# Output product of each attention block in two parts, a halved PSUM copy and an earlier first row transfer

## The chip, the cores and the metric

The kernel runs on one core of one Trainium2 chip. The metric is device time in microseconds of one execution: 1679.77 us, the median of three runs (1678.62 to 1679.84). Five engines appear in the profile: PE (matrix products; PEld is its weight load), DVE (vector engine), ACT (scalar engine), POOL (GpSimd) and SP, which only issues transfers.

## The reference

For x of 2048 rows and 512 columns, 32 heads of 16, and an inner width F of 1792:

```python
x = A_x
mod = (_silu(c) @ w_mod).reshape(c.shape[0], 6, 1, -1)
sa, ca, ga, sb, cb, gb = (mod[:, 0], ..., mod[:, 5])
h = _layernorm(x, axis=-1) * (1 + ca) + sa
x = x + ga * _A_ref(h, A_wqkv, A_wo)      # softmax attention over all rows, then @ wo
h = _layernorm(x, axis=-1) * (1 + cb) + sb
x = x + gb * _B_ref(h, B_w1, B_b1, B_w2)  # dense, bias, h * tanh(softplus(h)), dense
return x
```

## The kernel before

Every fp32 operand of a large product is split into a high and a low part, and three products (high with high, high with low, low with high) stand for one. The query rows are taken in four blocks of 512. The attention is a loop of **steps** t, written by hand: 16 steps per group of heads, 128 per block, 512 in all, with a prologue of 20. A filled step holds, for PE:

- four score products (L519), each followed by an exponential on ACT (L527);
- four products of the head group 20 steps ahead (L478), whose row maxima DVE takes (L480); they are the number that softmax subtracts;
- the product of probabilities and values of two steps before (L547), written as eight matmuls that I call *pv*; the profile shows them as one row with x8;
- up to six half products (64 of the 128 contraction rows, L132) of one **unit** of other work, each run beside a score or a maximum product in the other half of the array.

The units wait in a first-in first-out queue (L1104), each with a time from which it may start; `next_part` (L1110) hands six half products to each step, or three in the last 20 steps, where no maxima are left. `h` in the code counts half steps. A block qb has these units, which run during the steps of the block after it:

- *wo* i = 0 to 3: the attention's output product of 128 rows, 12 products, thus 24 halves or four steps. The result lies in the single bank "ms". `fin` (L832 to L850) copies it to the single buffer `yd` on ACT (L834), POOL adds it to row tile y (L835), and three half steps later the layer norm begins (`norm_y`, L702): a mean pass on ACT over y with an accumulated sum (L708), a squared pass (L712) two half steps on, small POOL operations (L709, L713, L714) and the normed tile on POOL (L715).
- *tr* i: the transposition of that normed tile by eight small PE matmuls behind pv (L856). ACT copies its result out of PSUM (L861), POOL scales and shifts it (L864, four operations) and splits it (L95, L98) into `h`.
- *up* f = 0 to 13: the first dense product; it needs all four `h` tiles. A chain on ACT, DVE and POOL forms the activation and splits it.
- *down* (group, i): the second dense product over a group of f. ACT or DVE copies to `yd` (L906), POOL adds it to y (L907). Group 4 of a block runs between the next block's *wo* and *up* units.

The last query block has no loop behind it. Its output product, layer norm and dense layers stand in the **tail** (L1004 to L1095), which PE reads in order: the output product (L1020), then *down* units of the third block that were **held** for this place (L126 products into two ring banks, DVE adds them at L903), transpositions of the four normed tiles (L1055), the scale, shift and split of these (L719, L95, L98), more held units, and then up and down products alternating. Ten *down* units are held: six of them before the transpositions.

A further transfer concerns the start: the negated maxima of a head group are transposed (L497), copied by ACT (L500, L501), added by POOL (L502), and `put` (L504 to L511) issues four SP transfers of them to `qa`, which the score products read.

## Time and profile before

| quantity | value |
|---|---|
| median of three runs | 1679.77 us (1678.62 to 1679.84) |
| the profiled execution's own time | 1677.17 us |
| its span in the trace | 1675.4 us |
| granted PE clock | 1.00 |
| PE busy, share of the span | 1649.3 us, 98% |
| DVE busy | 1425.7 us, 85% |
| ACT busy | 1336.4 us, 80% |
| POOL busy | 910.9 us, 54% |

The profile gives each engine's busy time, the chain of work that ended last, groups of instructions by line, and a timeline. In a timeline a row starts with the time in us from the span's start and the duration in us; then follow engine, line, operation, destination and sources, and the number of merged instructions. A bracket at the end gives the engine's idle time before the row and what ended it. Matmul ends are modelled and overlap their successors, so the length of a step is read from the start of one pv row to the start of the next.

### The profile page before, as it was taken

The numbers are of one execution on the slowest core, as the hardware profiler recorded it, in microseconds if no ns is written. First come the engines' busy times: TensorE is split into PE (matmuls) and PEld (weight loads), VectorE is DVE, ScalarE is ACT, GpSimd is POOL, SyncE is SP. The second block draws the span as 40 slices with busy tenths as digits, with TensorE's granted clock in tenths as the row PEclk, the third lists the DMA queues.
The fourth block names the chain that finished last, engine by engine and source line by source line (L and its number), as shares of the span: only waits on it lengthen the run. The fifth ranks groups of instructions, "written<-read, shape, count | busy, mean of one in ns | idle before, by whom it ended". The sixth has DMA issues, their size and how long they took to land.

```text
span 1675.4 us, 33101 instructions
## 1 busy us (share of the span) xinstructions
PE 1649.3 (98%) x12316; PEld 921.4 (55%) x12316; DVE 1425.7 (85%) x2327; ACT 1336.4 (80%) x2625; POOL 910.9 (54%) x938
## 2 busy tenths in 40 slices
PE   7999999999999999999999999999999999999999
PEld 5755665555435455555555555555555555554687
DVE  6888898888998988888888888888888888882577
ACT  6257778787779899888889898888889889889364
POOL 5155215465434398854535498654535597645532
PEclk9999999999999999999999999999999999999999
DMA  7677456777684443435343644334442645332362
GB/s 253 186 224 226 110 168 198 236 229 226 201 254 113 111 107 86 119 78 160 86 126 75 200 105 97 102 108 121 121 102 72 178 104 134 87 116 84 126 228 73
DMA packets 113992, 240.03 MB, mean 143 GB/s; under 512 B 24048, under 2 KB 49648, under 8 KB 107784
## 3 DMA queue, kind: packets, MB, share of 16 engines
q1 hardware_dynamic: 113832, 237.92, 50.4%
q8 instruction: 97, 1.59, 0.4%
q14 instruction: 63, 0.52, 0.1%
HBM read 179.95 MB, written 51.44 MB: 138 GB/s over the span
## 4 chain that ended last, share of the span: by engine, by line
PE 83%; POOL 5%; DMA 4%; ACT 4%; DVE 2%; SPq 1%; issue 1%; ACTq 0%; DVEq 0%; POOLq 0%
PE bk L547 27%; PE ring L478 22%; PE ring L519 21%; PE bk L132 6%; PE ring L126 2%; ACT pr L527 2%; PE ring L1088 2%; DMA ka<-kscr 1%; PE bk L126 1%; DVE mx L480 1%; DMA wr<-in_A_wqkv 1%; DMA xt<-in_A_x 1%; POOL rr L781 1%; POOL ee L779 1%; POOL hb L786 1%
## 5 line engine op out<-in xcount | busy, mean ns | idle before, releaser
L480 DVE TENSOR_REDUCE mx<-ring 128x1 f32<-128x512 f32 x2048 | 1278.8, 684 | 159.5 <-PE bk L132 96.0
L527 ACT ACTIVATE pr<-ring 128x512 f32<-128x512 f32 x2048 | 1087.8, 603 | 197.9 <-PE bk L132 159.8
L478 PE MATMUL ring<-ka,qa 64*128 64x512 f32 x2048 | 773.9, 425 | 1.5 <-ACT pr L527 0.8
L519 PE MATMUL ring<-qa,ka 64*128 64x512 f32 x2048 | 719.3, 395 | 6.6 <-ACT pr L527 4.9
L478 PEld LDWEIGHTS ring<-ka,qa 64*128 64x128 f32 x2048 | 365.9, 184 | 396.0 <-DVE mx L480 351.6
L547 PE MATMUL bk<-pr,vg 128*32 128x512 f32 x4096 | 545.1, 604 | 0.0
L519 PEld LDWEIGHTS ring<-qa,ka 64*128 64x128 f32 x2048 | 374.3, 184 | 113.8 <-ACT pr L527 37.7
L132 PE MATMUL bk<-h,w 64*128 64x512 f32 x1008 | 279.9, 409 | 0.0
L132 PE MATMUL bk<-w,a_h 64*128 64x512 f32 x576 | 194.7, 417 | 1.2 <-ACT pr L527 0.6
L132 PEld LDWEIGHTS bk<-h,w 64*128 64x128 f32 x1008 | 171.5, 184 | 2.9 <-ACT yd L906 0.9
L547 PEld LDWEIGHTS bk<-pr,vg 128*32 128x32 f32 x4096 | 80.9, 108 | 127.2 <-issue 120.0
L132 PE MATMUL bk<-w,a_l 64*128 64x512 f32 x288 | 113.9, 396 | 0.0
L749 POOL TENSOR_SCALAR ee<-hb 128x512 f32<-128x512 f32 x42 | 62.5, 1488 | 93.6 <-ACT hb L743 85.1
L132 PEld LDWEIGHTS bk<-w,a_h 64*128 64x128 f32 x576 | 95.4, 185 | 5.3 <-ACT pr L527 1.8
L779 POOL TENSOR_TENSOR ee<-ee,rr 128x512 f32<-128x512 f32 x42 | 54.0, 1285 | 75.5 <-ACT rr L770 75.3
L132 PE MATMUL bk<-w,o_hl 64*128 64x512 f32 x288 | 79.5, 408 | 0.0
L98 POOL TENSOR_TENSOR a_l<-hb,a_h 128x512 fp32r<-128x512 f32 x53 | 71.7, 1354 | 4.4
L907 POOL TENSOR_TENSOR y<-yd,y 128x512 f32<-128x512 f32 x40 | 51.5, 1287 | 28.2 <-ACT yd L906 28.0
L502 POOL TENSOR_TENSOR mt<-mt,mh 32x128 fp32r<-32x128 f32 x32 | 14.4, 450 | 87.9 <-ACT mh L501 87.9
L132 PE MATMUL bk<-h_h,wl 64*128 64x512 f32 x168 | 56.8, 418 | 0.0
L787 POOL TENSOR_TENSOR hb<-hb,rr 128x512 f32<-128x512 f32 x42 | 54.5, 1298 | 3.3
L764 POOL TENSOR_TENSOR ee<-ee,rr 128x512 f32<-128x512 f32 x42 | 54.0, 1287 | 3.5
(211 smaller groups left out, 1847.9 us busy)
## 6 DMA issues: line engine op xcount, KB each, us to landing
ka<-kscr SPq DMA_DIRECT2D x124, 384.0 KB
w<-w2scr SPq DMA_DIRECT2D x56, 512.0 KB
w<-w1scr SPq DMA_DIRECT2D x46, 512.0 KB
vg<-vscr SPq DMA_DIRECT2D x32, 552.0 KB
qa<-qscr SPq DMA_DIRECT2D x124, 100.0 KB
kscr<-qh SPq DMA_DIRECT2D x16, 512.0 KB
qscr<-qh SPq DMA_DIRECT2D x32, 256.0 KB
w1scr<-hl SPq DMA_DIRECT2D x14, 512.0 KB
```

The source lines that it names most:

```text
L98: (nc.gpsimd if eng == "p" else nc.vector).tensor_sub(lo, src, hi.bitcast(F32))
L132: i = nc.tensor.matmul(acc, l[64 * g:64 * g + 64], r[64 * g:64 * g + 64], start=start, stop=stop)
L478: nc.tensor.matmul(pm, qt[64 * s:64 * s + 64, qs * P:(qs + 1) * P], kt[64 * s:64 * s + 64, kb * TB:(kb + 1) * TB], start=True, stop=True)
L480: return nc.vector.tensor_reduce(out=mxs[n][:, s, 4 * j + qs, kb:kb + 1], in_=pm, op=ALU.max, axis=AX.X)
L519: nc.tensor.matmul(p_, kt[64 * s:64 * s + 64, kc * P:(kc + 1) * P], qt[64 * s:64 * s + 64, :], start=True, stop=True)
L527: e = nc.scalar.activation(pr, p_, AF.Exp, scale=SCALE)
L547: nc.tensor.matmul(accs[n][32 * h:32 * h + 32, :], vgs[n][:, o:o + 32], pts.pop((t, h)), start=(kc == 0), stop=(kc == 15))
L749: nc.gpsimd.tensor_scalar_min(buf("ee", 2), b["hb"], HCAP)
L764: nc.gpsimd.tensor_mul(ee, ee, rr)
L779: nc.gpsimd.tensor_mul(ee, ee, rr)
L787: nc.gpsimd.tensor_mul(hb, hb, rr)
L907: nc.gpsimd.tensor_add(y[i], yd, y[i])
```

## The change

Five edits, in three groups:

1. **The output product in two parts.** A unit `part(i)` takes the contraction tiles 0 and 1, and `wo(i)` the tiles 2 and 3. The four `part` units stand in the queue behind *down*(4,0) and ahead of the four `wo` units, and may start before the block's last heads are done. Each part has its own copy on ACT, which also accumulates a row sum (L830), and its own add on POOL (L831). The row mean comes from these sums and from the stored mean of x (POOL, L832), so the mean pass L708 of before is gone; the squared pass follows three half steps after the copy of `wo(i)`, and *tr* 1 to 3 wait for 7 half steps from it as before, *tr* 0 for 5.
   As a consequence every *up* and *down* unit of blocks 0 to 2 stands 8 steps earlier in the loop: block 0's *up* 0 at step 150 instead of 158, block 1's at 278 instead of 286, block 2's at 406 instead of 414. The number of steps ahead of the last 20 without any half product falls from 28 to 20, and *down*(2,2) and *down*(2,3) of the third block move from the tail into steps 496 to 511. The tail holds eight units, five ahead of the transpositions.
2. **The copy of a transposed tile** is halved: DVE copies the first 64 rows of the tile, ACT the rest.
3. **The first heads' rows**: for the first head group the add stands on DVE instead of POOL, and `put` one half step earlier. A row load of y moves from 20 to 11 half steps behind *down*(4,0).

```diff
-    def norm_y(y):
...
-        def mean():
-            nc.scalar.activation(xn, y, AF.Identity, accum_out=ss[:, 0:1])
-            nc.gpsimd.tensor_scalar(ss[:, 1:2], ss[:, 0:1], -1.0 / D, 0.0, op0=ALU.mult, op1=ALU.add)
...
+    def norm_y(y, ss):
+        xn = mst["p"].tile([P, D], F32, tag="hb", name="xn2", bufs=3)
+        nc.scalar.activation(xn, y, AF.Square, bias=ss[:, 1:2], accum_out=ss[:, 2:3])
...
-        def wo_unit(i, tag):
+        def wo_unit(i, tag, ks):
...
-                nc.scalar.copy(yd, acc)
+                nc.scalar.activation(yd, acc, AF.Identity, accum_out=part)
                 nc.gpsimd.tensor_add(y[i], yd, y[i])
...
+                nc.gpsimd.tensor_scalar(m, part, -1.0 / D, xmean[:, 4 * qb + i:4 * qb + i + 1] if ks[0] == 0 else ss[i][:, 0:1],
+                                        op0=ALU.mult, op1=ALU.add)
+                if ks[0] == 0:
+                    return
...
-                nc.scalar.copy(hf.rearrange("p k (g m) -> p g k m", g=2),
-                               acc[:, :, :256].rearrange("p g (k m) -> p g k m", k=DK))
+                for g, eng in enumerate((nc.vector.tensor_copy, nc.scalar.copy)):
+                    eng(hf[:, :, 64 * g:64 * g + 64], acc[:, g, :256].rearrange("p (k m) -> p k m", k=DK))
...
-                    load(h + 20, then["y"], lambda j: load_y(qb + 1, j), range(3, 4))
+                    load(h + 11, then["y"], lambda j: load_y(qb + 1, j), range(3, 4))
...
+        def part(i):
+            queue(lambda: 0 if qb else done.get("w", 4 * T) + 4, lambda tag: wo_unit(i, tag, range(2)))
+
         def wo(i):
-            queue(lambda: max(t0, done.get("w", 0 if qb else 4 * T)), lambda tag: wo_unit(i, tag))
+            queue(lambda: t0, lambda tag: wo_unit(i, tag, range(2, DK)))
...
-            mst["held"] = lambda j, acc: down_unit(2 + (j + 2) // 4, (j + 2) % 4, None, acc)
+            mst["held"] = lambda j, acc: down_unit(3 + j // 4, j % 4, None, acc)
...
+            for i in range(4):
+                b["units"]["part"](i)
...
-        nc.gpsimd.tensor_add(mt, mc, mh.bitcast(F32))
+        (nc.gpsimd if n else nc.vector).tensor_add(mt, mc, mh.bitcast(F32))
...
-        at(2 * (16 * n + 16 - PRO) + 3, put)
+        at(2 * (16 * n + 16 - PRO) + (3 if n else 2), put)
...
-        fins = held((4, 5))
+        fins = held((4,))
...
-        for js in ((6, 7), (8, 9)):
+        for js in ((5, 6), (7,)):
```

Three places show the order of instructions. First ACT, in block 1's attention loop's following stage, before the change, behind the copy of the first *wo* result (`yd`; `pr` are exponentials, `xn` and `ln_s` the norm's tiles, `y_5280` the row tile):

```order
L834 COPY yd<-bk 128x512
L527 ACTIVATE pr_0_1175<-ring 128x512
L527 ACTIVATE pr_0_1182<-ring 128x512
...
L708 ACTIVATE xn_9910,ln_s<-y_5280 128x512
L527 ACTIVATE pr_1_1183<-ring 128x512
L527 ACTIVATE pr_2_1177<-ring 128x512
L527 ACTIVATE pr_2_1184<-ring 128x512
L527 ACTIVATE pr_2_1151<-ring 128x512
L712 ACTIVATE xn_9910,ln_s<-y_5280,ln_s 128x512
```

The same place after the change, from the copy of one `wo` result to that of the next:

```order
L830 ACTIVATE yd,ln_s<-bk 128x512
L529 ACTIVATE pr_1_1177<-ring 128x512
L529 ACTIVATE pr_1_1184<-ring 128x512
...
L529 ACTIVATE pr_2_1178<-ring 128x512
L706 ACTIVATE xn_9943,ln_s<-y_5281,ln_s 128x512
L529 ACTIVATE pr_2_1185<-ring 128x512
L830 ACTIVATE yd,ln_s<-bk 128x512
```

The mean pass is gone, and the squared pass of one tile stands a single exponential ahead of the copy of the next tile's result. Next POOL in the same stage, before, from the add of the second tile (`gate_97` serves as a row tile) to that of the third:

```order
L835 TENSOR_TENSOR gate_97<-yd,gate_97 128x512
L864 TENSOR_SCALAR hf_10008<-hf_10008,modc 128x128 x4
L95 TENSOR_SCALAR h_9994<-hf_10008 128x4x128
L98 TENSOR_TENSOR h_9995<-hf_10008,h_9994 128x4x128
L709 TENSOR_SCALAR ln_s<-ln_s 128x1
L713 TENSOR_SCALAR ln_s<-ln_s 128x1
L714 TENSOR_TENSOR ln_s<-ln_s,nhalf 128x1
L715 TENSOR_SCALAR xn_10052<-gate_97,ln_s 128x512
L835 TENSOR_TENSOR gate_98<-yd,gate_98 128x512
```

And after the change, from the add of the third tile to that of the fourth:

```order
L831 TENSOR_TENSOR gate_99<-yd,gate_99 128x512
L832 TENSOR_SCALAR ln_s<-ln_s 128x1
L862 TENSOR_SCALAR hf_10055<-hf_10055,modc 128x128 x4
L96 TENSOR_SCALAR h_10045<-hf_10055 128x4x128
L99 TENSOR_TENSOR h_10046<-hf_10055,h_10045 128x4x128
L707 TENSOR_SCALAR ln_s<-ln_s 128x1
L708 TENSOR_TENSOR ln_s<-ln_s,nhalf 128x1
L709 TENSOR_SCALAR xn_10100<-gate_99,ln_s 128x512
L831 TENSOR_TENSOR y_5277<-yd,y_5277 128x512
```

POOL has the same sequence per tile as before, but the `wo` results now arrive every two steps instead of every four. Last DVE in the tail, before, behind the last normed tile (`pr`); L903 is the add of a held unit, L98 the low part of `h`:

```order
L109 TENSOR_SCALAR pr_1_1158<-pr_0_1157,ln_mv,ln_rs 128x512
L903 TENSOR_TENSOR y_5279<-ring,y_5279 128x512
L903 TENSOR_TENSOR y_5280<-ring,y_5280 128x512
...
L903 TENSOR_TENSOR y_5279<-ring,y_5279 128x512
L903 TENSOR_TENSOR y_5280<-ring,y_5280 128x512
L98 TENSOR_TENSOR h_17796<-hf_17829,h_17795 128x512
```

And after:

```order
L110 TENSOR_SCALAR pr_1_1159<-pr_0_1158,ln_mv,ln_rs 128x512
L901 TENSOR_TENSOR y_5278<-ring,y_5278 128x512
L901 TENSOR_TENSOR y_5279<-ring,y_5279 128x512
L901 TENSOR_TENSOR y_5280<-ring,y_5280 128x512
L901 TENSOR_TENSOR y_5281<-ring,y_5281 128x512
L901 TENSOR_TENSOR y_5278<-ring,y_5278 128x512
L99 TENSOR_TENSOR h_17901<-hf_17928,h_17900 128x512
```

Five adds of held units instead of six stand between the last normed tile and the first low part of `h`. SP's order of transfers is the same in both kernels, at the start too.

More of the change, by code (lines that the diff above doesn't have):

```diff
@@ L827, in wo_unit @@
             s = slice(i * P, (i + 1) * P)
-            seq = [(l[:, k, s], wos[k][:, v, :]) for k in range(DK) for l, v in ((oh, 0), (oh, 1), (ol, 0))]
+            seq = [(l[:, k, s], wos[k][:, v, :]) for k in ks for l, v in ((oh, 0), (oh, 1), (ol, 0))]
             for j, (l, r) in enumerate(seq):
@@ L833, in fin, with spread @@
                 yd = mst["p"].tile([P, D], F32, tag="yd", name="yd", bufs=1)
-                nc.scalar.copy(yd, acc)
+                if ks[0] == 0:
+                    ss[i] = mst["p"].tile([P, 4], F32, tag="ln_s", name="ln_s", bufs=4)
+                m, part = (ss[i][:, j:j + 1] for j in ((0, 2) if ks[0] == 0 else (1, 3)))
+                nc.scalar.activation(yd, acc, AF.Identity, accum_out=part)
                 nc.gpsimd.tensor_add(y[i], yd, y[i])
-                def mean():
-                    xn[i], first, then = norm_y(y[i])
-                    first()
-                    at(h + 5, then)
-                at(h + 3, mean)
-                done["xn", i] = h + 7
+                nc.gpsimd.tensor_scalar(m, part, -1.0 / D, xmean[:, 4 * qb + i:4 * qb + i + 1] if ks[0] == 0 else ss[i][:, 0:1],
+                                        op0=ALU.mult, op1=ALU.add)
+                if ks[0] == 0:
+                    return
+                def spread():
+                    xn[i] = norm_y(y[i], ss[i])
+                at(h + 3, spread)
+                done["xn", i] = h + (7 if i else 5)
                 if i == 3 and qb == 0:
@@ L944, in block @@
         if qb == NB - 2:
-            mst["held"] = lambda j, acc: down_unit(2 + (j + 2) // 4, (j + 2) % 4, None, acc)
+            mst["held"] = lambda j, acc: down_unit(3 + j // 4, j % 4, None, acc)
         return {"wo": wos, "y": y, "w1": w1s, "w2": w2s, "loads": first_loads,
-                "units": {"wo": wo, "up": up, "down": down}}
+                "units": {"wo": wo, "part": part, "up": up, "down": down}}
     def all_blocks():
@@ L976, in all_blocks @@
             up(13)
+            down(2, 2)
+            down(2, 3)
             if qb < NB - 2:
[L978 to L979 removed]
                 for i in range(4):
```

25 lines of the change are left out of this document (10 added, 15 removed).

## Prediction

> **What bounds the kernel.** I read the page first: the busy line, the chain that ended last, then the cost of one exponential.
>
> ```profile
> PE 1649.3 (98%) x12316; PEld 921.4 (55%) x12316; DVE 1425.7 (85%) x2327; ACT 1336.4 (80%) x2625; POOL 910.9 (54%) x938
> PE 83%; POOL 5%; DMA 4%; ACT 4%; DVE 2%; SPq 1%; issue 1%; ACTq 0%; DVEq 0%; POOLq 0%
> L527 ACT ACTIVATE pr<-ring 128x512 f32<-128x512 f32 x2048 | 1087.8, 603 | 197.9 <-PE bk L132 159.8
> ```
>
> PE is busy for nearly the whole span and carries 83% of the chain. But an average hides stages with different limits, so I took the windows view for three: steps without half products, filled steps, and the last 20 steps.
>
> ```profile
> 440.00:480.00 40.00, 36.52 (x234) 14.19 (x232) 36.66 (x62) 30.66 (x62) 6.20 (x7) 1.00 0.83 241
> 1440.00:1480.00 40.00, 40.00 (x314) 21.46 (x310) 35.88 (x61) 34.54 (x70) 22.65 (x21) 1.00 0.27 75
> 1520.00:1560.00 40.00, 39.15 (x274) 15.94 (x277) 2.87 (x5) 39.08 (x78) 24.41 (x24) 1.00 0.24 87
> ```
>
> The columns behind the length are the busy us of PE, PEld, DVE, ACT and POOL, then clock, DMA share and GB/s. In the empty steps DVE's maxima set the pace (36.66 of 40) and PE has gaps (36.52). In the filled ones PE has none (40.00 of 40), while ACT still has 5.5 us. In the last 20 steps PE and ACT are both full (39.15 and 39.08), and DVE is free. The clock is 1.00 in all three. What a step costs, empty and filled, comes from pv rows, ten steps apart each:
>
> ```profile
> 438.79 1.07 PE L547 MATMUL bk<-pr,vg 128*32 128x512 f32 x8
> ...
> 466.23 1.07 PE L547 MATMUL bk<-pr,vg 128*32 128x512 f32 x8
> ...
> 1443.15 1.06 PE L547 MATMUL bk<-pr,vg 128*32 128x512 f32 x8
> ...
> 1471.47 1.07 PE L547 MATMUL bk<-pr,vg 128*32 128x512 f32 x8
> ```
>
> An empty step takes (466.23 − 438.79)/10 = 2.744 us, a filled one (1471.47 − 1443.15)/10 = 2.832 us. So six half products in an empty step cost only 0.088 us. The same work in the tail, where nothing runs beside it, costs its full time. That is the whole mechanism of the change.
>
> **Work moved out of the tail.** These are the rows of the tail.
>
> ```profile
> 1574.75 0.64 PE L126 MATMUL ring<-w,a_h 128*128 128x512 f32 x2
> ...
> 1581.41 0.55 DVE L109 TENSOR_SCALAR pr<-pr,ln_mv,ln_rs 128x512 f32<-128x512 f32 x1 [0.72 <-POOL ln_rs L107]
> 1581.87 2.48 DVE L903 TENSOR_TENSOR y<-ring,y 128x512 f32<-128x512 f32 x4
> ...
> 1585.92 0.60 PE L1055 MATMUL ring<-ident,pr 128*128 128x128 f32 x4
> ...
> 1587.23 0.60 PE L1055 MATMUL bk<-ident,pr 128*128 128x128 f32 x4
> ...
> 1591.69 0.69 DVE L98 TENSOR_TENSOR h<-hf,h 128x512 fp32r<-128x512 f32 x1 [0.51 <-POOL h L95]
> ...
> 1593.25 2.89 PE L126 MATMUL bk<-h,ka 128*128 128x512 f32 x12
> ```
>
> Six held units, 48 products, fill 1574.75 to 1585.92: 0.2327 us each. Two units of 12 products leave, so PE could come out 24 × 0.2327 = 5.6 us sooner. But something else is late next. With 30 products left, PE reaches the transpositions at 1574.75 + 30 × 0.2327 = 1581.7. They need the last normed tile, from DVE at 1581.41 + 0.55 = 1581.96, and a ring bank, which the first held add returns at 1581.87 + 2.48/4 = 1582.5. So they start at 1582.5, 0.8 us after PE is ready. They take 1587.23 − 1585.92 = 1.3 us to the last one's start and some 0.4 more, and then 18 products 4.2 us: the first up product starts at 1588.4 instead of 1593.25, a gain of 4.85. The split of `h` took from 1585.92 to 1591.69 + 0.69 = 1592.38, 6.46 us behind the transpositions' start; from 1582.5 that is 1588.96, and five held adds of 0.62 (to 1585.0) may push it 0.3 further, to 1589.3. Only the last three of twelve products need that last low part, so it should be covered; if it isn't, the gain is 3.9. I take **−4.7**, between −3.5 and −5.6.
>
> The 24 products become 48 halves: eight empty steps less (28 to 20), at 0.088: **+0.7**. The last 20 steps hold three halves each in both kernels, so they cost the same.
>
> **Twelve more evictions, a pass less.** Each wo result now comes out in two parts.
>
> ```profile
> L834 ACT COPY yd<-bk 128x512 f32<-128x512 f32 x12 | 7.1, 591 | 0.0
> ...
> 843.26 0.59 ACT L906 COPY yd<-bk 128x512 f32<-128x512 f32 x1
> ...
> 843.35 1.06 PE L547 MATMUL bk<-pr,vg 128*32 128x512 f32 x8
> ...
> 911.83 0.62 ACT L708 ACTIVATE xn<-y 128x512 f32<-128x512 f32 x1
> ...
> 912.41 1.06 PE L547 MATMUL bk<-pr,vg 128*32 128x512 f32 x8
> ...
> 912.92 0.59 ACT L906 COPY yd<-bk 128x512 f32<-128x512 f32 x1
> ...
> 915.46 1.06 PE L547 MATMUL bk<-pr,vg 128*32 128x512 f32 x8
> ```
>
> The copies last 0.59 us. One that starts with pv (843.26 beside 843.35) lies under pv's 1.06 us and costs nothing, since the bank is free before the next unit's first product. One that is late by 0.5 (912.92 beside 912.41, because a mean pass stood ahead of it) lengthened its step to 915.46 − 912.41 = 3.05, so +0.22. A copy that nothing hides at all costs its 0.59; twelve of them 7.1, which is rival D below. In ACT's total the change is no load: 12 copies more, 12 mean passes of 0.62 less. But the squared passes now stand an exponential ahead of the next copy, as in that row. If the nine copies that follow such a pass (wo 1 to 3 in three blocks), and the twelve first parts besides, were all late like that, it would be 21 × 0.22 = 4.6; if none, 0. I take the nine, **+2.0**.
>
> The Trainium skill, "TensorEngine Tiling (Array Packing)", section "PSUM Bottleneck", says that tiling speeds TensorE but not the emptying of PSUM, which may then become the bottleneck, and advises to use both ScalarE and VectorE for it. This kernel runs its units in half the array, so by that rule the twelve added copies would be exposed. The row at 843.26, a copy that costs nothing, speaks against it.
>
> **POOL behind the parts.** Per tile POOL works as these rows say.
>
> ```profile
> L835 POOL TENSOR_TENSOR y<-yd,y 128x512 f32<-128x512 f32 x10 | 12.8, 1283 | 37.9 <-ACT yd L834 37.9
> ...
> 885.37 1.75 POOL L864 TENSOR_SCALAR hf<-hf,modc 128x128 f32<-128x128 f32 x4 [0.35 <-ACT hf L861]
> ...
> 887.21 0.62 POOL L95 TENSOR_SCALAR h<-hf 128x512 fp32r<-128x512 f32 x1
> 887.91 1.29 POOL L98 TENSOR_TENSOR h<-hf,h 128x512 fp32r<-128x512 f32 x1
> ...
> L714 POOL TENSOR_TENSOR ln_s<-ln_s,nhalf 128x1 f32<-128x1 f32 x12 | 6.7, 560 | 1.0
> L715 POOL TENSOR_SCALAR xn<-y,ln_s 128x512 f32<-128x512 f32 x10 | 7.7, 774 | 1.1
> ```
>
> 1.28 + 1.75 + 0.62 + 1.29 + 0.56 + 0.77 = 6.3, with some 1.1 for two small operations and the gaps between (887.21 to 887.91 holds 0.08 idle): 7.4 us a tile. Before, a tile came every four steps, over 11.3 us; now every two, 5.7 us. So POOL falls about 1.6 us behind per tile, and in blocks 1 and 2 three further adds of 1.28 (down group 4) mix in. By this count the high part of the fourth tile is ready about 0.7 us after the slot of up 0 in those two blocks: **+1.4**, between 0 and 4.
>
> **DVE's half copies.**
>
> ```profile
> L861 ACT COPY hf<-ring 128x512 f32<-128x512 f32 x12 | 7.1, 588 | 0.8 <-PE ring L856 0.6
> L562 DVE COPY ot<-bk 128x256 f32<-128x256 f32 x32 | 13.6, 424 | 6.9 <-PE bk L547 6.9
> ```
>
> DVE gets twelve copies of 256 columns, 0.42 us each, 5.1 in all; by the first windows DVE has about 4 us free in 40 of filled steps, so most is covered. ACT gains 0.2 on each. I take **+0.6**, between −0.5 and 2.
>
> **Weights and first rows.**
>
> ```profile
> 468.65 0.39 SPq L675 DMA_DIRECT2D w<-woscr x1
> ...
> 96.38 1.27 POOL L98 TENSOR_TENSOR wl<-wr,wh 128x512 fp32r<-128x512 f32 x1
> ...
> 97.68 0.38 SPq L214 DMA_DIRECT2D wr<-in_A_wqkv  x1
> ...
> 102.87 0.47 PE L519 MATMUL ring<-qa,ka 64*128 64x512 f32 x1 [0.99 <-DMA qa<-mt]
> ```
>
> In block 0 the first part begins behind the pv at 466.23 (step 125's) and needs wo tile 1 by about 468. The last of the four loads was issued at 468.65, and tile 1's two loads ahead of it, with the DMA engines 0.83 busy in that window. If it lands a little late PE stands: **+0.4**, 0 to 1. The first score product waits 0.99 us for the moved rows. But SP keeps its order: these transfers stand behind a load issued at 97.68, which waits for a buffer that POOL frees at 96.38 + 1.27 = 97.65. An earlier add and an earlier `put` cannot pass it: **0**, at best −0.99.
>
> **Waits that move.** Eight steps' shift changes which POOL and ACT work meets.
>
> ```profile
> 836.95 1.06 PE L547 MATMUL bk<-pr,vg 128*32 128x512 f32 x8
> ...
> 837.97 0.59 ACT L906 COPY yd<-bk 128x512 f32<-128x512 f32 x1 [1.01 <-POOL y L907]
> ...
> 840.51 1.06 PE L547 MATMUL bk<-pr,vg 128*32 128x512 f32 x8
> ...
> 619.53 0.63 ACT L755 ACTIVATE ee<-ee 128x512 f32<-128x512 f32 x1 [0.30 <-POOL ee L749]
> ```
>
> Here ACT stood 1.01 us for `yd`, since POOL's add came late, and the step took 840.51 − 836.95 = 3.56, +0.73. Two blocks have that step, 1.4 in all; the wait of 0.30 for POOL comes in the like unit of each of three, 0.9. After the shift those units meet POOL elsewhere. I take **−2.3**, both gone, between −4 and 0: a new meeting may cost what the old one did.
>
> **Sum.** −4.7 + 0.7 + 2.0 + 1.4 + 0.6 + 0.4 + 0 − 2.3 = −1.9, so 1675.3 for the profiled execution of 1677.17. That execution is 2.6 us (0.15%) under the median of the three runs, 1679.77; applied to the median, the forecast is **1677.9**.
>
> **The rivals.**
>
> *A: everything but the tail is hidden.* The copies lie under pv like the one at 843.26, POOL keeps up, the old waits go. Then −4.7 + 0.7 − 2.3 = −6.3: 1673.5. For it: ACT has 5.5 us free in 40, POOL 17. Against: POOL's 7.4 us a tile against 5.7.
>
> *B, slower: POOL holds `yd`.* There is one `yd`, and with results every two steps its add must be over when the next copy is due. If POOL's queue is later than the row at 837.97, that is, if the copy starts over 1.0 us after pv's start, each copy costs 0.73 and no exponential passes it on ACT. Copies behind a busy POOL are wo 1 to 3 in three blocks and down(4,1) to (4,3) in two: 15 × 0.73 = 11.0, in place of 2.0 + 1.4. Then −1.9 − 3.4 + 11.0 = +5.7: 1685.5. For it: the 1.6 us of lag per tile add up to 6 over four tiles, more than the slack. Against: the add itself stands ahead of the tile's scaling and split in POOL's order, and the first parts' adds come before any of that.
>
> *C: the first rows do come sooner,* if the wait at 102.87 hangs on the add and not on SP's order: −0.99 more, 1676.9. It lies within the forecast's own range. That the edit on them does nothing is what I expect.
>
> *D: the added copies are bare.* Each of the twelve delays the next unit's first product by its own length: 7.1 in place of 2.0, a sum of +3.2, 1683.0. For it: bank "ms" is single, so a product of the next unit cannot start before the copy. Against: pv lies between the two. This is what the rule of "PSUM Bottleneck" in the Trainium skill would make of the change.
>
> **Chances and range.** Forecast with C: 0.48; A: 0.30; B: 0.16; D: 0.06. A measurement of this kernel can tell about 0.2%, 3.4 us, from no change: 1676.4 to 1683.1. The forecast's own range is 1674.5 to 1681 (tail at either end, the rest within a few us); about 0.07 of its 0.48 falls under 1676.4. A is faster, but if the old waits stay it is not: 0.02 of it. B is slower, and so is half of D, which lies at the bound, 0.03 of 0.06; 0.01 of B may be milder. So faster 0.35, same 0.41 + 0.02 + 0.03 + 0.01 = 0.47, slower 0.18. The range that leaves 2 in 10 out goes from A with the tail's full 5.6 (1672.6) to 1684.5, past D and over the milder part of B.
>
> **What would show it.** The first L126 product with `h` in the tail should start 1.5 to 3 us earlier than 1593.25, being the sum of −4.85 and what the loop adds; pv to pv, the steps of the copies show +0.2 (forecast), 0 (A) or +0.7 with a bracket that names POOL's add (B). The fourth tile's split on POOL ahead of or behind up 0 shows the POOL term (L519's first bracket: rival C). I am wrong if the filled step itself changes from 2.832, or if a term stands in a stage that I haven't named.

## The result, and the profile after

The changed kernel takes 1682.61 us (median of 19 runs, 1680.68 to 1685.4) against 1680.00 us for the kernel before in the same sessions (19 runs, 1677.13 to 1683.4). The ratio is 1.0017, with a 95% interval of 1.001 to 1.0023: some 2.9 us slower, where 1.9 us faster was forecast. The time lies in the stated range, on the other side of no change. The profiled execution took 1682.26 us, its span 1680.5 us.

The page's busy line and the chain of the changed kernel:

```profile
PE 1654.5 (98%) x12340; PEld 927.1 (55%) x12340; DVE 1427.8 (85%) x2338; ACT 1334.7 (79%) x2639; POOL 929.9 (55%) x963
PE 88%; ACT 3%; DVE 2%; POOL 1%; DMA 1%; issue 1%; SPq 0%; ACTq 0%; DVEq 0%; POOLq 0%
```

ACT is busy 1.7 us less, PE 5.2 us more. Totals like these don't show where 3 us went. Lengths of steps do. I took the start of every pv in both traces and compared step by step. The differences stand in few places, the same in each block:

| place | changed minus before, us | forecast, us |
|---|---|---|
| start of the trace to the first pv | +2.06 | 0 |
| step 68 (with 12 and 84 it differs from one execution of a kernel to the next) | +0.7 | none |
| steps 116 to 135 without step 126 | +0.5 | +0.7 |
| step 126, wait for weights | +1.2 | +0.4 |
| output product and transpositions (steps 136 to 159, 264 to 289, 392 to 417) | +7.2 | +4.0 |
| old waits gone, new ones come | −2.3 | −2.3 |
| last pv to the first up product of the tail | −4.9 | −4.7 |
| the rest of the tail | +0.6 | 0 |
| all other steps together | +0.1 | 0 |

The fifth line holds the longer steps at 136 to 148, 268 to 276 and 396 to 404, less the transposition and mean pass steps of before that became plain ones. The sixth holds steps 256 and 384 (−0.72 and −0.69), 180, 308 and 436 (−0.53, −0.50, −0.55), 189, 317 and 445 (−0.41, −0.32, −0.29), and new waits: 0.44 to 0.45 at 193, 321 and 449, 0.14 and 0.19 at 300 and 428. The lines add up to the 5.1 us between the two spans, within rounding.

That is more than the 2.9 us between the medians, because the first, second and fourth lines differ between executions of one kernel: the first pv of the kernel before comes at 109.6 us in two profiles and at 111.8 in a third, and in the second profile of the changed kernel (run 13) step 68 takes 2.83 instead of 3.52 and step 126 takes 3.01 instead of 3.96. The fifth line recurs. Its steps add up to 219.0 to 219.1 us in four profiles with the stage of before (the kernel before three times and run 5) and to 226.1 to 226.2 in five with that of the changed kernel (that kernel twice, run 6, and the kernel of run 11 twice). So the stage is compared by step lengths below, to some 0.1 us.

First the tail, on PE, before the change and then after it. A row with x24 is the last three pv:

```profile
1558.73 2.78 PE L547 MATMUL bk<-pr,vg 128*32 128x512 f32 x24
...
1593.25 2.89 PE L126 MATMUL bk<-h,ka 128*128 128x512 f32 x12
1595.98 2.88 PE L126 MATMUL ring<-h,ka 128*128 128x512 f32 x12
```

```profile
1568.11 2.78 PE L549 MATMUL bk<-pr,vg 128*32 128x512 f32 x24
...
1591.74 0.66 PE L1058 MATMUL ring<-ident,pr 128*128 128x128 f32 x4 [0.48 <-DVE y L901]
...
1597.72 2.96 PE L127 MATMUL bk<-h,ka 128*128 128x512 f32 x12
1600.52 2.96 PE L127 MATMUL ring<-h,ka 128*128 128x512 f32 x12
```

The transpositions wait for DVE's first held add, as the bracket says, and the first up product starts 1597.72 − 1568.11 = 29.6 us behind the start of the last three pv, where it was 1593.25 − 1558.73 = 34.5 before: −4.9. Then an up unit takes 1600.52 − 1597.72 = 2.80 us, where the kernel before needed 1595.98 − 1593.25 = 2.73.

Now the stage between a block's output product and its first up unit, block 1, PE and ACT. L549 is pv, L706 the squared pass, L830 the copy of a wo result, L860 the half copies, L854 the transpositions:

```profile
878.09 1.07 PE L549 MATMUL bk<-pr,vg 128*32 128x512 f32 x8
...
881.32 1.06 PE L549 MATMUL bk<-pr,vg 128*32 128x512 f32 x8
884.17 1.07 PE L549 MATMUL bk<-pr,vg 128*32 128x512 f32 x8
885.17 0.47 PE L854 MATMUL ring<-ident,xn 64*128 64x64 f32 x8
886.00 0.50 PE L480 MATMUL ring<-ka,qa 64*128 64x512 f32 x1 [0.37 <-ACT pr L529]
...
887.85 1.06 PE L549 MATMUL bk<-pr,vg 128*32 128x512 f32 x8
```

```profile
877.51 0.71 ACT L706 ACTIVATE xn<-y,ln_s 128x512 f32<-128x512 f32 x1
...
878.21 0.58 ACT L529 ACTIVATE pr<-ring 128x512 f32<-128x512 f32 x1
878.69 0.59 ACT L830 ACTIVATE yd<-bk 128x512 f32<-128x512 f32 x1
...
885.34 1.09 ACT L529 ACTIVATE pr<-ring 128x512 f32<-128x512 f32 x2
886.30 0.40 ACT L860 COPY hf<-ring 128x256 f32<-128x256 f32 x1
```

The copy at 878.69 starts 0.6 us behind its pv (878.09) because the squared pass stands ahead of it, and this step takes 881.32 − 878.09 = 3.23 instead of 2.83. With a transposition in it, the step takes 887.85 − 884.17 = 3.68. The like step of before, with its transposition (L856):

```profile
883.17 1.06 PE L547 MATMUL bk<-pr,vg 128*32 128x512 f32 x8
884.17 0.47 PE L856 MATMUL ring<-ident,xn 64*128 64x64 f32 x8
...
886.27 1.07 PE L547 MATMUL bk<-pr,vg 128*32 128x512 f32 x8
```

It took 886.27 − 883.17 = 3.10. In the changed kernel PE's first product behind the transpositions waits for a bank that a late exponential frees. The copy of the tile is halved here, but the halves do not run together:

```profile
885.73 0.42 DVE L860 COPY hf<-ring 128x256 f32<-128x256 f32 x1 [0.32 <-PE ring L854]
```

DVE ends at 886.15, ACT begins at 886.30. ACT still has exponentials to do when DVE ends, so these rows alone don't show that ACT's half waits for DVE's; run 3 does.

Three smaller points. The halves of the output product of block 0 meet weights that are late. Ten steps later they wait for POOL, which splits the last heads' result:

```profile
471.83 0.50 PE L133 MATMUL bk<-w,o_hl 64*128 64x512 f32 x1 [0.64 <-DMA w<-woscr]
...
501.01 0.49 PE L133 MATMUL bk<-w,o_hl 64*128 64x512 f32 x1 [0.20 <-POOL o_hl L99]
```

The second of these rows lies in step 136, which takes 3.29 us instead of 2.84. Third, the first rows' add is done earlier, but their transfer and the first score product are not:

```profile
96.60 0.67 DVE L504 TENSOR_TENSOR mt<-mt,mh 32x128 fp32r<-32x128 f32 x1
...
104.93 0.47 PE L521 MATMUL ring<-qa,ka 64*128 64x512 f32 x1 [1.18 <-DMA qa<-mt]
```

The add ends at 97.27, and the trace up to here runs 2 us later than that of before; so it is 2.8 us sooner in its place. The score product's wait is 1.18 us, no shorter than the 0.99 of before.

### The profile page after: what moved, and what is told of

The parts are those of the page before. It is cut to its first block, busy times and chain, and to the rows that moved or that the text cites. A ratio compares the mean times of both kernels' runs of the same rounds, so it can differ in the third digit from the quotient of the medians.

```text
span 1680.5 us, 33217 instructions
## 1 busy us (share of the span) xinstructions
PE 1654.5 (98%) x12340; PEld 927.1 (55%) x12340; DVE 1427.8 (85%) x2338; ACT 1334.7 (79%) x2639; POOL 929.9 (55%) x963
## 4 chain that ended last, share of the span: by engine, by line
PE 88%; ACT 3%; DVE 2%; POOL 1%; DMA 1%; issue 1%; SPq 0%; ACTq 0%; DVEq 0%; POOLq 0%
PE bk L549 29%; PE ring L480 23%; PE ring L521 20%; PE bk L133 10%; PE bk L127 3%; PE ring L127 2%; PE ring L1091 2%; ACT pr L529 2%; DVE mx L482 1%; DMA kscr<-ql 0%; DMA w<-woscr 0%; PE bk L1023 0%; PE ring L499 0%; PE ring L1023 0%; ACT yd L830 0%
## 5 line engine op out<-in xcount | busy, mean ns | idle before, releaser
L549 PE MATMUL bk<-pr,vg 128*32 128x512 f32 x4096 | 545.1, 604 | 0.0
L133 PE MATMUL bk<-w,a_h 64*128 64x512 f32 x608 | 205.6, 418 | 0.9 <-ACT pr L529 0.8
L549 PEld LDWEIGHTS bk<-pr,vg 128*32 128x32 f32 x4096 | 81.0, 108 | 128.0 <-issue 120.9
L133 PE MATMUL bk<-w,a_l 64*128 64x512 f32 x304 | 119.5, 393 | 0.0
L133 PEld LDWEIGHTS bk<-w,a_h 64*128 64x128 f32 x608 | 100.3, 185 | 4.8 <-ACT pr L529 1.8
L133 PEld LDWEIGHTS bk<-w,a_l 64*128 64x128 f32 x304 | 56.0, 184 | 4.6
```

The source lines that it names most:

```text
L133: i = nc.tensor.matmul(acc, l[64 * g:64 * g + 64], r[64 * g:64 * g + 64], start=start, stop=stop)
L549: nc.tensor.matmul(accs[n][32 * h:32 * h + 32, :], vgs[n][:, o:o + 32], pts.pop((t, h)), start=(kc == 0), stop=(kc == 15))
```

## The experiments

Theories, in the order in which they came. **P**: the squared pass one exponential ahead of a wo result's copy delays that copy. **H**: the two halves of the tile's copy run one behind the other and hold what follows. **L**: ACT is simply full over the two steps between wo results, wherever its work stands. **M**: P and H lie on each other, so that each hides the other. **A**: the 64 bytes per partition that the stored means take move every later tile, and this slows the start and the tail; its rival **S** is the start's own edit or chance. Each run's ratio is to the kernel before on the same chip; the changed kernel stands at 1.0017.

### 1. The whole copy on ACT again

```diff
-                for g, eng in enumerate((nc.vector.tensor_copy, nc.scalar.copy)):
-                    eng(hf[:, :, 64 * g:64 * g + 64], acc[:, g, :256].rearrange("p (k m) -> p k m", k=DK))
+                nc.scalar.copy(hf.rearrange("p k (g m) -> p g k m", g=2),
+                               acc[:, :, :256].rearrange("p g (k m) -> p g k m", k=DK))
```

> The changed kernel with ACT copying the whole transposed tile again, as before the change; all else changed. Theory H (the two halves run one behind the other, since ACT's half waits for DVE's, and hold the exponentials behind them): the last transposition steps of each block, 3.41 to 3.53 us in the changed kernel, go back to 3.09, and the twelve together give 3 to 4 us. Theory P (what costs is the squared pass one exponential ahead of the next copy of a wo result): the steps of 3.68 stay within 0.1, the kernel gains less than 1 us. Theory L (ACT is simply full over the two steps between wo results): 0.1 to 0.2 us more ACT work per tile, so 1 to 2 us slower.

Measured: 1.0005 (0.9995 to 1.0015). The last transposition step of a block goes from 3.41 to 3.09, as H said, but the 3.68 us steps become 3.71, and the third of blocks 1 and 2 3.89, so the stage gains only 0.3 us over the three blocks. P's prediction held for the first two 3.68 us steps of a block, and H's for the last ones, but not H's 3 to 4 us for the twelve. The median's gain, 2.0 us by the ratios, is larger than the step lengths give; the wait for weights was absent in this profile.

### 2. The squared pass two half steps sooner

```diff
-                at(h + 3, spread)
+                at(h + 1, spread)
```

> The changed kernel with the squared pass one half step behind the copy of the wo result instead of three, so three exponentials behind that copy and five ahead of the next one; PE's order is the same. Theory P: the copies start with pv again, the 3.22 us steps go to 2.84 and the 3.68 us steps lose about 0.4; nine such neighbours, so 3 to 4 us faster. Theory L: the same work in the same two steps, within 1 us of the changed kernel. Theory H: within 1 us. A wait of the squared pass for POOL's add would show as a bracket on ACT and make it slower.

Measured: 1.0002 (0.9993 to 1.001). The 3.23 us step goes to 2.84, but its neighbour grows by 0.24; the 3.68 us steps go to 3.43, and in blocks 1 and 2 one neighbour grows by 0.43; there ACT waits 0.51 us for POOL ahead of the squared pass. In all 1.3 us over the blocks (2.5 by the ratios): between P's 3 to 4 and the 1 us that L allowed.

### 3. The halved copy alone, in the kernel before

```diff
-                nc.scalar.copy(hf.rearrange("p k (g m) -> p g k m", g=2),
-                               acc[:, :, :256].rearrange("p g (k m) -> p g k m", k=DK))
+                for g, eng in enumerate((nc.vector.tensor_copy, nc.scalar.copy)):
+                    eng(hf[:, :, 64 * g:64 * g + 64], acc[:, g, :256].rearrange("p (k m) -> p k m", k=DK))
```

> The kernel before with nothing changed but the halved copy of the transposed tile. Theory H: ACT's half starts when DVE's has ended, and the transposition steps of 3.09 us become about 3.4: 2 to 4 us slower than before. Theories P and L: DVE and ACT share the copy, nothing or up to 1 us faster.

Measured: 1.0023 (1.0015 to 1.0032), 3.9 us slower. Eleven of the twelve transposition steps are 0.27 to 0.34 longer, one 0.40, together 4.0, and no other step behind the first twelve moves by more than 0.12. One of them, PE, then DVE, then ACT:

```profile
887.06 1.07 PE L547 MATMUL bk<-pr,vg 128*32 128x512 f32 x8
...
890.49 1.06 PE L547 MATMUL bk<-pr,vg 128*32 128x512 f32 x8
```

```profile
888.62 0.42 DVE L862 COPY hf<-ring 128x256 f32<-128x256 f32 x1 [0.38 <-PE ring L856]
```

```profile
889.13 0.37 ACT L862 COPY hf<-ring 128x256 f32<-128x256 f32 x1 [0.60 <-PE ring L519]
```

The step takes 890.49 − 887.06 = 3.43, and ACT, free 0.60 us, starts 0.09 behind DVE's end (889.04). The bracket names a product of PE, but in all twelve tiles ACT's half starts 0.09 us behind the end of DVE's, with ACT free for 0.5 to 1.2 us ahead of it. So half a copy on each engine takes as long as 0.42 + 0.09 + 0.37 = 0.88, against 0.59 for the whole. H is shown for the kernel before.

### 4. Block 0's first parts two steps later

```diff
-            queue(lambda: 0 if qb else done.get("w", 4 * T) + 4, lambda tag: wo_unit(i, tag, range(2)))
+            queue(lambda: 0 if qb else done.get("w", 4 * T) + 8, lambda tag: wo_unit(i, tag, range(2)))
```

> The changed kernel with the first block's four first parts two steps later (steps 128 to 135 instead of 126 to 133), behind the landing of the weights. If the 1.23 us by which step 126 is longer is the wait for wo tile 1 alone, it goes and nothing else moves: 1.1 to 1.3 us faster than the changed kernel. Rival: the parts then run into something else (the copies meet the first group's work of POOL at steps 134 to 137), and less than 0.5 is left.

Measured: 1.002 (1.0011 to 1.0028). Step 126 goes back to 2.73, but step 138 takes 3.66 instead of 2.84. As the rival said, the copies run into POOL's other work. This is ACT there:

```profile
509.83 0.60 ACT L830 ACTIVATE yd<-bk 128x512 f32<-128x512 f32 x1 [1.03 <-POOL y L831]
```

It is the wait for `yd` that rival B of the prediction priced at 0.73 a time; it costs 0.83 here, and it is absent from the changed kernel itself.

### 5. A spare 64 bytes in the kernel before

```diff
     modc = cst.tile([P, 4, DK], F32, name="modc")
+    spare = cst.tile([P, NKC], F32, name="spare")
```

> The kernel before with one spare constant tile of 64 bytes per partition that nothing uses, at the place where the change puts the stored means; every later tile moves by 64 bytes. Theory A (the start and the tail's up products are slower in every profile with the stored means since the tiles behind them lie 64 bytes further on): the second matmul group of the start comes about 2.64 us behind the first instead of 2.47, the 16 small matmuls behind it take 3.6 us instead of 1.95, the first score product is 2 us later, and 12 up products in the tail take 2.79 us instead of 2.72; 2 to 3 us slower than before. Rival S (the edit in the first normalization's statistics does it, or chance): the start and the tail as in the kernel before, no difference.

Measured: 1.0011 (1.0003 to 1.002), 1.8 us slower, by a tile that nothing reads or writes. The start on PE, first of the kernel before, then with the spare tile; L390/L391 are the two matmul groups that wait for the modulation weights, L396/L397 the 16 small ones:

```profile
9.99 1.94 PE L390 MATMUL ring<-wma,sil 128*32 128x512 f32 x8 [9.99 <-DMA wma<-in_w_mod]
12.45 1.83 PE L390 MATMUL ring<-wma,sil 128*32 128x512 f32 x8 [0.53 <-DMA wma<-in_w_mod]
14.21 1.95 PE L396 MATMUL ring<-sel,row 128*128 128x1 f32 x16
```

```profile
10.81 1.94 PE L391 MATMUL ring<-wma,sil 128*32 128x512 f32 x8 [10.81 <-DMA wma<-in_w_mod]
13.48 1.93 PE L391 MATMUL ring<-wma,sil 128*32 128x512 f32 x8 [0.73 <-DMA wma<-in_w_mod]
15.34 3.58 PE L397 MATMUL ring<-sel,row 128*128 128x1 f32 x16
```

The second group comes 2.67 us behind the first instead of 2.46, and the 16 matmuls take 3.58 instead of 1.95. From pv's last start to the end the tail is 0.4 us longer, with 2.80 for the first up units. All the places that A named, at a smaller total.

### 6. A pad ahead of the start's weights, in the changed kernel

```diff
+        pad = lp.tile([P, 112], F32, name="pad")
         wma = [lp.tile([P, DK, D], F32, name=f"wma{i}") for i in range(2)]
```

> The changed kernel with a pad of 448 bytes per partition ahead of the two modulation weight tiles of the start, so that these and the tiles of that pool behind them lie 512 bytes further on than in the kernel before. Theory A, if it is the place of these tiles relative to 512 bytes that counts: the second matmul group again 2.47 us behind the first, the first score product about 2 us sooner than in the changed kernel, the tail unchanged; 1.5 to 2 us faster than the changed kernel. Rival S: no difference to the changed kernel.

Measured: 1.0019 (1.001 to 1.0028), nothing gained. The windows from 12 to 14 us, of the changed kernel and with the pad:

```profile
12.00:14.00 2.00, 1.55 (x8) 0.20 (x8) 0.00 (x0) 1.14 (x2) 0.00 (x0) 1.00 1.14 325
```

```profile
12.00:14.00 2.00, 1.47 (x11) 0.20 (x8) 0.00 (x0) 1.31 (x3) 0.00 (x0) 1.00 1.13 373
```

The transfer rate goes from 325 back to 373 GB/s (379 in the kernel before), and the gap ahead of the second group to 0.53 us. But the 16 matmuls still take 3.58 us. So the place of the tiles sets the gap; the gap alone does not make the start fast.

### 7. The whole copy on DVE

```diff
-                for g, eng in enumerate((nc.vector.tensor_copy, nc.scalar.copy)):
-                    eng(hf[:, :, 64 * g:64 * g + 64], acc[:, g, :256].rearrange("p (k m) -> p k m", k=DK))
+                nc.vector.tensor_copy(hf.rearrange("p k (g m) -> p g k m", g=2),
+                                      acc[:, :, :256].rearrange("p g (k m) -> p g k m", k=DK))
```

> The changed kernel with the transposed tile copied by DVE alone. Theory L (ACT is full over the two steps between wo results): ACT loses 0.4 us and the wait for DVE's half per tile, and the transposition steps of 3.68 go to 3.3 to 3.4; with DVE's 0.7 us beside its maxima of 2.5 per step, 2 to 4 us faster than the changed kernel. Rival: DVE is then what is full, since 2.5 + 0.7 is more than a step of 3.09, and the gain is under 1 us.

Measured: 1.0015 (1.0006 to 1.0024). Not one step in blocks 1 and 2 moves by more than 0.12. ACT without the copy is no help, so L in its plain form falls; the rival, that DVE is then full, fits the same result and was not told apart from M.

### 8. The squared pass over 64 columns

```diff
-        nc.scalar.activation(xn, y, AF.Square, bias=ss[:, 1:2], accum_out=ss[:, 2:3])
+        nc.scalar.activation(xn[:, :64], y[:, :64], AF.Square, bias=ss[:, 1:2], accum_out=ss[:, 2:3])
```

> The changed kernel with the squared pass over 64 of the 512 columns: it leaves out seven eighths of the sum of squares that the second layer norm divides by. ACT loses about 0.45 us per tile. Theory L: the steps of 3.22 and 3.68 lose 0.2 to 0.45 each, 1 to 1.5 us per block, 3 to 4.5 us faster than the changed kernel. Rival (the excess is the wait of ACT's half copy for DVE and nothing else): the steps stay within 0.1 and the gain is under 1 us.

Measured: 0.9998 (0.9989 to 1.0007), 3.2 us faster than the changed kernel by the ratios. The steps lose 0.21 to 0.37 each, 1.1 us per block in blocks 1 and 2. The 3.68 us steps stop at 3.41 to 3.44: what the halves alone made of the transposition steps in run 3. That is where M comes from: with the squared pass out of the way the halves' wait holds the step.

### 9. The halves by columns

```diff
-                for g, eng in enumerate((nc.vector.tensor_copy, nc.scalar.copy)):
-                    eng(hf[:, :, 64 * g:64 * g + 64], acc[:, g, :256].rearrange("p (k m) -> p k m", k=DK))
+                for a, eng in ((0, nc.vector.tensor_copy), (2, nc.scalar.copy)):
+                    eng(hf[:, a:a + 2].rearrange("p k (g m) -> p g k m", g=2),
+                        acc[:, :, 64 * a:64 * a + 128].rearrange("p g (k m) -> p g k m", k=2))
```

> The changed kernel with the copy of the transposed tile halved by its columns (DVE the first two of four column tiles, ACT the other two) instead of by its rows, so that the two halves write separate stretches of the target. Theory H1 (ACT's half waits for DVE's because their targets interleave): the two halves run side by side, the last transposition steps of each block go from 3.41 to 3.1, and the 3.68 us steps, which the squared pass holds too, lose 0.1 to 0.3; 1 to 3 us faster than the changed kernel. Rival H2 (ACT's half waits for DVE's whatever they write): all steps as in the changed kernel.

Measured: 1.0021 (1.0011 to 1.0031). H2: ACT's half still starts 0.03 to 0.19 us behind DVE's end, in all twelve tiles, and the steps of the stage stay within 0.1. The wait does not hang on targets that interleave. In the halves by rows each engine reads a bank of its own (`acc[:, g]`), so it doesn't hang on both engines reading one bank either. What the two splits share is the target tile and the pair of banks; which of these matters was not tried.

### 10. The whole copy and the early squared pass together

The edits of runs 1 and 2.

> The changed kernel with ACT copying the whole transposed tile, and with the squared pass one half step behind the copy of the wo result: the two edits that gave 0.3 and 1.3 us in step lengths when made alone. Theory M (two waits of the same height lie on each other, so each edit alone uncovers the other): together the 3.68 us steps go to 3.1 to 3.4, 1.5 to 2 us per block, 4.5 to 6 us faster than the changed kernel. Theory L (ACT is full over the two steps between wo results, wherever its work stands): no more than 1.5 us.

Measured: 0.9994 (0.9985 to 1.0003), 3.9 us faster than the changed kernel by the ratios. The same stage of block 1 on PE, and on ACT the wait that is left:

```profile
885.24 1.06 PE L549 MATMUL bk<-pr,vg 128*32 128x512 f32 x8
...
888.34 1.07 PE L549 MATMUL bk<-pr,vg 128*32 128x512 f32 x8
```

```profile
894.61 0.72 ACT L706 ACTIVATE xn<-y,ln_s 128x512 f32<-128x512 f32 x1 [0.82 <-POOL ln_s L832]
```

The step of 3.68 takes 888.34 − 885.24 = 3.10. The three blocks gain 1.34, 1.13 and 1.18 us in steps, 3.7, where the two edits apart gave 0.3 and 1.3. M is shown by the step lengths: each wait hid the other. The medians can't show it: by the ratios the edits gave 2.0 and 2.5 us apart and 3.9 together, each known to some 2 us. The gain is also less than the 4.5 to 6 us that M was given, and the stage is still 3.5 us longer than in the kernel before. Part of what is left is the squared pass of the fourth tile, which now waits 0.82 us for POOL's add and mean; POOL's lag, which the prediction feared for `h`, appears there.

### 11. The changed kernel at the old addresses

```diff
-    nhalf = cst.tile([P, 1], F32, name="nhalf")
-    nc.gpsimd.memset(nhalf, -0.5)
-    two = cst.tile([P, 1], F32, name="two")
-    nc.gpsimd.memset(two, 2.0)
-    hcap = cst.tile([P, 1], F32, name="hcap")
+    vals = cst.tile([P, 4], F32, name="vals")
+    nhalf, two, hcap = (vals[:, j:j + 1] for j in range(3))
+    nc.gpsimd.memset(nhalf, -0.5)
+    nc.gpsimd.memset(two, 2.0)
     nc.gpsimd.memset(hcap, HCAP)
```

> The changed kernel with three one-column constants put into one tile, which gives back the 64 bytes per partition of the stored means: every later tile lies where it lay in the kernel before. Theory A: the second matmul group of the start 2.47 us behind the first, the 16 small matmuls behind it 1.95 us instead of 3.6, the first score product 2 us sooner, 12 up products in the tail 2.72 us instead of 2.79; 2 to 2.6 us faster than the changed kernel, so within 1 us of the kernel before. Rival S: start and tail as in the changed kernel, nothing gained.

Measured: 1.0002 (0.9993 to 1.0011), 2.5 us faster than the changed kernel by the ratios, the size that A gave, known to some 2 us. In its profile the gap is 0.54, and two up units take 2.72 and 2.73 us before the third takes longer:

```profile
1596.97 2.89 PE L126 MATMUL bk<-h,ka 128*128 128x512 f32 x12
1599.69 2.89 PE L126 MATMUL ring<-h,ka 128*128 128x512 f32 x12
1602.42 2.95 PE L126 MATMUL bk<-h,w 128*128 128x512 f32 x12
```

The tail is 0.4 us shorter than in the changed kernel. The 16 small matmuls, though, took 3.58 us in this execution: the part of A on the fast start did not show here.

### 12. All three together

The edits of runs 1, 2 and 11.

> The addresses of the kernel before, the whole copy on ACT and the early squared pass in one kernel. Theories A and M: 2 to 2.6 and 4.5 to 6 us off the changed kernel, 4 to 6 us faster than the kernel before. A and L: 0.5 to 1.5 us faster than before. S and M: 2 to 3 us faster than before. S and L: 1 to 2.5 us slower.

Measured: 0.9983 (0.9974 to 0.9992), 1677.25 us against 1679.71: 2.9 us faster than the kernel before, so faster than both. It is less than the 4 to 6 us of A and M together and lies where S and M were put, 2 to 3 us. The places still speak for both A and M: the stage is 3.7 us shorter than in the changed kernel, as in run 10, and the tail 0.4 us, as in run 11. What A is worth at the start stays uncertain. The start here was a fast one:

```profile
11.94 1.93 PE L391 MATMUL ring<-wma,sil 128*32 128x512 f32 x8 [0.54 <-DMA wma<-in_w_mod]
13.79 1.95 PE L397 MATMUL ring<-sel,row 128*128 128x1 f32 x16
```

### 13. How often the start is fast

The kernel before twice, the changed one once, the kernel of run 11 once, one execution each.

> The kernel before once more. Theory A (the longer gap between the first two matmul groups, which the 64 bytes cause, keeps the clock down): gap 0.53, the 16 small matmuls in 1.95 us. Rival S (chance of the execution): as often 3.58 as 1.95.

> As the run ahead of it: 1.95 us for the 16 small matmuls by theory A, either by rival S.

> The changed kernel once more. Theory A: gap 0.70, the 16 small matmuls in 3.58 us. Rival S: as often 1.95 as 3.58.

> The changed kernel with the addresses of before once more, whose first profile had the short gap and the late clock. Theory A with a chance in it (the short gap allows the early clock, the long one doesn't): gap 0.54, and either 1.95 or 3.58. Rival S: the same, so this run alone counts only as one more draw at the short gap.

Measured: 1.95 us for the 16 matmuls in the first, 3.58 in the second at the same gap:

```profile
12.80 1.94 PE L390 MATMUL ring<-wma,sil 128*32 128x512 f32 x8 [0.54 <-DMA wma<-in_w_mod]
```

The changed kernel had a gap of 0.75 and 3.58, run 11's kernel 0.54 and 3.58. Over all profiles: with a gap of 0.53 to 0.55 the start is fast in four of eight, with 0.70 to 0.79 in none of ten. If gap and fast start had nothing to do with each other, the four fast ones would all fall to the short gap about once in 44 times; so the link is likely, and not certain. On average the first pv comes at 111.1 us in the seven profiles with the addresses of before and at 112.6 in the ten with the 64 bytes, with up to 3.3 us between executions of one group. So of the 2.06 us between the two profiles that were compared some 1 to 1.5 us, an estimate from these numbers, belongs to the change on average, and the rest to the draw.

## Why the prediction was wrong

**The tail** was right in its mechanism and size: −4.9 up to the first up product, where −4.85 was worked out and −4.7 taken, with DVE's first held add as the late one. The 0.6 that the up products lost behind it was not in the sum: 0.4 of it goes with the addresses (runs 5 and 11).

**Filled steps** (+0.5 for +0.7) were right. **The waits that move** came out at −2.3, as forecast, but the match is partly luck. The two steps with a wait of ACT for `yd` are gone (−1.4, as priced), and the three at 180, 308 and 436 (−1.6 for −0.9). Three more that the sum didn't name went too (−1.0), and new ones of +1.7 came, which it had put at nothing.

**The halved copy** is the step of the sum that failed: it was put at +0.6 with "most is covered" by DVE's free time. What counted was not DVE's load but that ACT's half starts behind DVE's, with the exponentials behind it. Run 3 measured 4.0 us in the kernel before. The trace of before had shown it. That kernel already splits another copy, `ot`, over the two engines; the prediction took its 0.42 us from DVE's row and did not use ACT's, which names what ACT waits for:

```profile
L563 ACT COPY ot<-bk 128x256 f32<-128x256 f32 x32 | 12.0, 374 | 9.4 <-DVE ot L562 5.1 <-ACT pr L527 2.8 <-DMA w2scr<-hl 0.6
```

```profile
1561.63 0.42 DVE L562 COPY ot<-bk 128x256 f32<-128x256 f32 x1 [2.23 <-PE bk L547]
1562.09 0.37 ACT L563 COPY ot<-bk 128x256 f32<-128x256 f32 x1 [1.88 <-DVE ot L562]
```

In all 32 pairs of before, ACT's half of `ot` starts 0.03 to 0.08 us behind the end of DVE's.

**Evictions and POOL** were put at +2.0 and +1.4. With the halved copy these make up the 7.2 us of the stage, where 4.0 was forecast for the three. The terms are not additive, which the sum took for granted: put into the kernel before, the halves cost 4.0 us (run 3); taken out of the changed kernel alone, they give back 0.3 (run 1); and with both the halves and the late squared pass gone, 3.5 us are left (run 10). The place was right: a copy behind a squared pass is late and lengthens its step. Its size was not: 0.39 without a transposition instead of 0.22, and 0.58 with one. The copies of the twelve first parts, on the other hand, cost nothing: steps 128 to 133 take what filled steps take, and 258 to 263 keep their length. So the rule of the Trainium skill ("TensorEngine Tiling (Array Packing)", section "PSUM Bottleneck") has its point here only for copies that stand beside another ACT pass, and its advice to empty PSUM with both engines, followed by halving the copy of one tile, made this kernel slower by run 3, 0.33 us a tile. POOL, which was feared for `h`, held PE up in another place, step 136 (+0.45): there it has the add of the fourth first part ahead of the split of the last heads' result; that this add is the cause was not tried. Otherwise nothing in the stage waits for POOL in the changed kernel; with the squared pass sooner ACT does (0.51 us in run 2, 0.82 in run 10).

**Weights**: +0.4 was taken with 1 as its upper end. It is no constant: step 126 took between 2.83 and 3.96 us in most profiles of kernels with early parts, 5.1 and 6.2 in two; over the twelve profiles that is 0.8 us more than before on average.

**First rows**: 0, as forecast; the transfer keeps its place behind the load in SP's order.

**The start** was in no term. A constant of 64 bytes was read as costing nothing, and its addresses were not looked at. It costs some 1 to 1.5 us on average, by the profiles, and 2.06 between the two that were compared. The median answers the same way: the spare tile alone makes the kernel before 1.8 us slower, giving the bytes back makes the changed kernel 2.5 us faster; the first is known to some 1.5 us, the second to some 2.

Of the rivals, B's wait for `yd` came only when the first parts were moved (run 4), at nearly its price; D's sum of +3.2 is near the measured one by luck, as its mechanism, bare copies of first parts, is refuted; A's −6.3 was not reached even with the edits of runs 10 and 11 together (run 12, −2.9). What stays open is why ACT's half waits, and which tile's place it is that slows the up products.

## What to carry to other kernels

Work that moves from a serial tail into half-empty steps keeps its gain, but what comes with it is paid in the stage where the moved work is now denser; take the two terms apart before summing them. When one edit in a stage gives nothing, make two at once: waits that lie on each other hide one another, and here 0.3 and 1.3 apart were 3.7 together. Splitting a copy over two engines paid nothing here, since the halves ran one behind the other; look at a split that the kernel already has before pricing a new one.

## What the runs showed of the hardware

PE begins slowly. The 16 small matmuls at 14 to 15 us take 1.95 or 3.58 us, four 128 by 128 transpositions behind them 0.60 or 1.06, with the clock column at 1.00 in both cases. In the fast case this changes 4 us behind PE's first matmul, in the slow one about 13 us behind it, as these rows of the changed kernel show, four equal products each:

```profile
21.06 2.05 PE L127 MATMUL ring<-h_h,wh 128*128 128x512 f32 x4
...
24.09 1.07 PE L127 MATMUL ring<-h_h,wh 128*128 128x512 f32 x4
```

The Trainium skill, "TensorE: Matmul & The Clock Gate", section "Part 1: The HAM clock gate (the "warmup" mystery)", says that the array runs at half its rate until it has been busy for about 3.4 us, and that the point varies between runs. The factor nearly agrees (3.58 to 1.95 is 1.8), and so does the fast case with its 4 us. The slow case does not: there PE has worked without a break since 12.45 us and still changes only about 10 us later. The runs add that the start was slow ten times in ten with a gap of 0.70 to 0.79 us between the first two groups, and four times in eight with 0.53 to 0.55.

A start address matters: with the destination tiles 64 bytes off, the transfers of the start ran at 325 GB/s instead of 379 between 12 and 14 us (316 to 327 in all ten such profiles), and a pad that made the shift 512 bytes brought 373 back (373 to 397 in the eight others). And 12 products of 512 columns took 2.80 us instead of 2.73 in the tail when every tile lay 64 bytes further on.
